# Blocks of four key tiles from the first head on, seven query products placed among the feed-forward groups, and the queries' scratch laid out by part

## The chip, the cores and the metric

The kernel runs on one core of a Trainium2 chip. The core has TensorE (PE, matmuls into PSUM), VectorE (DVE), ScalarE (ACT), GpSimd (POOL) and SyncE (SP), which here issues nearly all DMAs. Each engine runs its instructions in order and waits on semaphores for what others produce. The metric is the time of one execution on the device in microseconds (us), as a median over runs. The profile is of one further execution.

## The reference

The kernel computes a gated mix of an attention layer and a feed-forward layer over the same x (one batch, 2048 tokens, 512 features), all in float32:

```python
g = _sigmoid((x * gate_w).sum(-1, keepdims=True))
q = (x @ wq).reshape(B, S, 32, 16)      # 32 heads of 16
k = x @ wk;  v = x @ wv                 # one key and one value head, shared by all 32
p = softmax(einsum("bhqd,bkd->bhqk", q, k) * 16 ** -0.5)
a = einsum("bhqk,bkd->bhqd", p, v) -> (S, 512) @ wo
b = (silu(x @ w_gate) * (x @ w_up)) @ w_down      # hidden size 1792
out = g * a + (1 - g) * b
```

There is no mask. The output is 2048 x 512 in float32.

## The kernel before

**Precision.** Products in float32 are made of three matmuls: each operand is split into a high part of a shorter format and the rest (names ending in h and l), and hi x hi, hi x lo and lo x hi are summed in PSUM (`three`, L111). A weight tile arrives raw by DMA (`wraw`, two buffers), and POOL casts its high part (L107) and subtracts it (L108).

**Queries.** x is transposed into four chunks of 512 tokens (`XC[c]`, features on the partitions). A query product (m, c) multiplies columns 128 m to 128 m + 127 of wq, which are eight heads, with chunk c; there are 16. Of each result three parts are kept, the low part `ql`, the high part `qh` and a bound `qb` = kmax * |qh|, and written to a scratch in DRAM, `q_d` (L248). `load_head(h)` fetches one head's rows from there into `qs` (L665, L666): 128 partitions, that is twice four parts of 16 rows, for two halves of the query tokens, so that a score is one matmul per half with 64 rows (L680). For m = 0, ACT makes `qh` (L233) and `qb` (L234); for the others DVE makes all parts (L230 to L238). A reduction on DVE keeps each product's largest bound (L254).

**Three phases.** A setup transposes x, makes keys and values and the four query products of m = 0; head 0 gets its `qs` straight from them. `fill(GAP)` runs three more query products whole. The main phase follows, and then a tail with the feed-forward work that is left, the output projection with wo, and the sum.

**The main phase** is under a manual schedule: the order in which the code is written is the order on each engine. It goes through 512 units u, each one head and one of 16 key tiles. A unit has two scores S (each two matmuls into a PSUM tile `pss` of 128 x 1024, of which there are two buffers), the exponentials into `pt` (ACT, L688; of a score of kind "H", DVE copies one half out, L684, and ACT takes that half later), and a mix (L700: four matmuls, one per chunk of query tokens, that sum values and denominators in `po`; the profile records each as two). Between the scores stand steps F of other work, the jobs: a query product (12 steps), a gate or up product of one feed-forward tile and chunk (12), a down product of a group of tiles (15 or 12). A step is two matmuls with 64 rows each, the lower half of one job and the upper half of another (L192), which run side by side. `Halves` picks these jobs. What jobs leave to ACT and DVE stands in `ACTS` and `DEFER`, and `settle` or `block` runs it, `block` within a budget of DVE time.

**The order of units.** The first 32 units come in 16 blocks of two (four S, eight F, two units' mixes; `BEGIN`), since only three `pt` buffers fit beside the x chunks 2 and 3 and the weights of wq. When the last query product is done, these are given up (`open_acc`), and there are six buffers in two pools of three. One block of transition (`TURN`: ten scores, sixteen F) takes the order over to blocks of four units in the order of `STEPS`, with four units' mixes at the end of each.

**Jobs.** First the nine remaining query products, m by m; then for each chunk three groups of feed-forward tiles (5, 5 and 4), the gate and up products of a group interleaved with the down products of the group before. Gate and up weights are loaded for the next tile but one when a product ends. The first two of each, and the first group's down weights, are loaded ahead of the main phase (L785 to L790), on SP behind head 1's queries. Weights of the second chunk's pass are also stored split in `w_d` (L160) and read from there in later passes (L166).

Of the kernel before, what the change touches and what calls it, by code (L numbers as in the profile page):

```python
# [8 lines left out]
F32 = mybir.dt.float32  # L9
# [9 lines left out]
P = 128  # L19
# [27 lines left out]
PTB = 3  # L47
WRB = 2
BLOCK = 4
BEGIN = 16  # L50
STOP = 2
EARLY = 6
OUTS = (1, 2, 3, 0)
# [3 lines left out]
TURN = "SS" + "SFF" * 8  # L57
# [5 lines left out]
def tile_gated_mix(ctx, tc, x, wq, wk, wv, wo, w_gate, w_up, w_down, gate_w, out):  # L63
# [10 lines left out]
    q_d = dpool.tile([H, 3 * DH, S], F32, name="q_d")  # L74
# [19 lines left out]

    qpool = tc.alloc_tile_pool(name="qpool", bufs=1, side="right")
# [7 lines left out]
    ACC, PAIR = {}, []  # L103
# [19 lines left out]
    ACTS, DEFER, LOADS, HOLD, EVAC, FRESH = [], [], [], [], [], set()  # L123
# [87 lines left out]
    def load_wq(m):  # L211
        WQ[m] = load_split(wq_v[:, :, m * P:(m + 1) * P], f"wq{m}", 1, qpool)

    def query(m, c):
# [8 lines left out]

        def keep(ps):
            qh = wp.tile([P, CH], F32R, name="hh", bufs=7)
            ql = wp.tile([P, CH], F32R, name="hl", bufs=7)

            if m:
                qb = wp.tile([P, CH], F32, name="ht" if c % 2 else "hs", bufs=2)
                nc.vector.tensor_copy(qh, ps)  # L230
            else:
                qb = wp.tile([P, CH], F32R, name="hl" if c % 2 else "hh", bufs=7).bitcast(F32)
# [13 lines left out]
            def store():  # L246
                for j, part in enumerate(parts):
                    nc.sync.dma_start(q_d[m * HG:(m + 1) * HG, j * DH:(j + 1) * DH, cs], part.bitcast(F32))  # L248

            if m:  # L250
                store()
            else:
                STORES.append(store)
            nc.vector.tensor_reduce(top[:, t:t + 1], qb, axis=AX.X, op=ALU.max)  # L254

        return Job(3 * KD, lambda: m in WQ, terms, keep)

    def queries():
        jobs = [query(m, c) for m in range(1, KD) for c in range(NCH)]
        jobs[-1].after.append(open_acc)  # L260
        jobs[-1].after.append(lambda: nc.vector.tensor_reduce(top[:, KD * NCH:], top[:, :KD * NCH], axis=AX.X, op=ALU.max))
        return jobs

    def open_acc():
# [685 lines left out]
```

## Time and profile before

| | us |
| --- | --- |
| median of three runs (1341.17 to 1343.20) | 1342.19 |
| the profiled execution | 1340.92 |
| its span, first to last instruction | 1339.1 |
| TensorE busy in it | 1327.4 |
| ACT busy | 1069.0 |
| DVE busy | 710.3 |
| POOL busy | 220.3 |

A row of a timeline has start and duration in us, engine, line, operation, tiles (output, then inputs), partitions and shape, and in brackets how long the engine had been idle before and what released it. "x4" counts instructions that ran on without a gap. SPq is SP's queue: the duration there is that of the issue of a DMA, not of the transfer. The chain of waits is followed back from the last instruction; its rows are start, duration, and what ran. In a table by stretches a row has the stretch and its length, then busy time and instructions of PE, PE's weight loads, DVE, ACT and POOL, then the granted clock, the share of the 16 DMA engines in use, and GB/s.

### The profile page before, as it was taken

How to read it: one execution, taken by the hardware profiler on the slowest of the kernel's cores; microseconds unless marked ns; L12 is line 12 of the kernel's file. 1: busy time of each engine (PE TensorE's matmuls, PEld its weight loads, DVE VectorE, ACT ScalarE, POOL GpSimd, SP SyncE). 2: the span in 40 equal slices, each digit the busy share in tenths (PEclk: the TensorE clock that was granted, in tenths of full speed). 3: DMA queues.
4: the chain of work that ended last, by engine and by line, in shares of the span. 5: the costliest groups of instructions: out<-in, count | busy, mean ns of one | idle time of the engine just before them, and what ended most of it. 6: DMA issues, size and time to landing. Idle time of an engine off the chain costs nothing.

```text
span 1339.1 us, 26770 instructions
## 1 busy us (share of the span) xinstructions
PE 1327.4 (99%) x10743; PEld 769.7 (57%) x10743; DVE 710.3 (53%) x1221; ACT 1069.0 (80%) x1475; POOL 220.3 (16%) x228
## 2 busy tenths in 40 slices
PE   9999999999999999999999999999999999999998
PEld 7655555555555555555555555555555555555586
DVE  4555565465455555555555555455445565455442
ACT  4578888888888888888888888888888888888511
POOL 5141321152042141143020000000000000001223
PEclk9999999999999999999999999999999999999999
DMA  8455221131135372275162342243132342333154
GB/s 278 137 178 191 67 60 36 36 105 46 54 106 156 117 232 68 68 212 159 38 206 85 127 131 84 68 133 97 52 99 68 126 147 68 99 108 115 53 184 144
DMA packets 104178, 151.84 MB, mean 113 GB/s; under 512 B 12657, under 2 KB 43633, under 8 KB 102385
## 3 DMA queue, kind: packets, MB, share of 16 engines
q1 hardware_dynamic: 102320, 149.86, 36.4%
q8 instruction: 88, 1.44, 0.5%
q10 hardware_dynamic: 1728, 0.20, 0.1%
q14 instruction: 42, 0.34, 0.1%
HBM read 98.11 MB, written 51.38 MB: 112 GB/s over the span
## 4 chain that ended last, share of the span: by engine, by line
PE 98%; DVE 1%; ACT 1%; issue 0%; POOL 0%; DVEq 0%; ACTq 0%
PE pf L192 38%; PE po L700 34%; PE pss L680 21%; PE pf L117 4%; ACT pt L688 0%; PE pss L562 0%; PE po L549 0%; DVE xl L567 0%; PE pss L602 0%; DVE acc L345 0%; DVE hs L282 0%; POOL wul L108 0%; DVE wkv_l L108 0%; ACT xh L566 0%; DVE ot L464 0%
## 5 line engine op out<-in xcount | busy, mean ns | idle before, releaser
L688 ACT ACTIVATE pt<-pss 128x1024 f32<-128x1024 f32 (+1 forms) x1024 | 842.0, 876 | 177.7 <-PE pss L680 146.5
L684 DVE COPY pt<-pss 128x512 f32<-128x512 f32 x354 | 244.8, 691 | 421.4 <-PE pss L680 386.5
L700 PE MATMUL po<-pt,vaug 128*32 128x512 f32 x4096 | 467.6, 595 | 0.0
L680 PE MATMUL pss<-qs,ks 64*128 64x512 f32 x2048 | 402.4, 417 | 1.2 <-ACT pt L688 1.1
L680 PEld LDWEIGHTS pss<-qs,ks 64*128 64x128 f32 x2048 | 193.1, 184 | 218.7 <-ACT pt L688 183.5
L700 PEld LDWEIGHTS po<-pt,vaug 128*32 128x32 f32 x4096 | 119.2, 109 | 260.3 <-issue 255.2
L688 ACT ACTIVATE pt<-pt 128x512 f32<-128x512 f32 x354 | 195.7, 620 | 0.0
L192 PE MATMUL pf<-xh,wgl 64*128 64x512 f32 (+1 forms) x440 | 162.0, 391 | 0.0
L192 PE MATMUL pf<-xh,wgh 64*128 64x512 f32 (+1 forms) x440 | 160.8, 392 | 0.3
L192 PE MATMUL pf<-xl,wgh 64*128 64x512 f32 (+1 forms) x440 | 160.3, 390 | 0.0
L192 PE MATMUL pf<-xh,wuh 64*128 64x512 f32 (+1 forms) x440 | 158.3, 392 | 1.0 <-POOL wuh L107 0.5
L192 PE MATMUL pf<-xl,wuh 64*128 64x512 f32 (+1 forms) x440 | 158.1, 390 | 0.0
L192 PE MATMUL pf<-xh,wul 64*128 64x512 f32 (+1 forms) x440 | 157.1, 391 | 0.4 <-POOL wul L108 0.4
L192 PE MATMUL pf<-wdh,hl 64*128 64x512 f32 (+1 forms) x427 | 143.8, 390 | 0.0
L192 PE MATMUL pf<-wdh,hh 64*128 64x512 f32 (+1 forms) x427 | 143.3, 390 | 0.0
L192 PE MATMUL pf<-wdl,hh 64*128 64x512 f32 (+1 forms) x427 | 143.3, 390 | 0.0
L709 DVE RECIPROCAL rsb<-rsb 128x128 f32<-128x128 f32 x128 | 117.0, 935 | 10.1 <-issue 7.8
L447 POOL CAST xh<-wraw 128x512 fp32r<-128x512 f32 x4 | 2.9, 729 | 536.8 <-DMA wraw<-o_d 536.8
L192 PEld LDWEIGHTS pf<-xh,wgh 64*128 64x128 f32 (+1 forms) x440 | 78.5, 185 | 9.6 <-issue 1.3
L192 PEld LDWEIGHTS pf<-xh,wuh 64*128 64x128 f32 (+1 forms) x440 | 77.2, 185 | 9.7 <-issue 1.9
L192 PEld LDWEIGHTS pf<-xl,wgh 64*128 64x128 f32 (+1 forms) x440 | 78.5, 185 | 5.8
L192 PEld LDWEIGHTS pf<-xh,wgl 64*128 64x128 f32 (+1 forms) x440 | 78.5, 185 | 5.4
(158 smaller groups left out, 1361.5 us busy)
## 6 DMA issues: line engine op xcount, KB each, us to landing
qs<-q_d SPq DMA_DIRECT2D x62, 192.0 KB
wraw<-in_B_w_gate_dram SPq DMA_DIRECT2D x28, 256.0 KB
wraw<-in_B_w_up_dram SPq DMA_DIRECT2D x28, 256.0 KB
wraw<-in_B_w_down_dram SPq DMA_DIRECT2D x28, 256.0 KB
wgh<-w_d SPq DMA_DIRECT2D x28, 256.0 KB
wgl<-w_d SPq DMA_DIRECT2D x28, 256.0 KB
wuh<-w_d SPq DMA_DIRECT2D x28, 256.0 KB
wul<-w_d SPq DMA_DIRECT2D x28, 256.0 KB
```

Source lines behind the costliest of these rows:

```text
L117: nc.tensor.matmul(ps, a, b, start=(i == 0), stop=(i == n - 1))
L192: ins = nc.tensor.matmul(self.ps, a, b, start=(i == 0 and not half), stop=(last and half != 0))
L447: nc.gpsimd.tensor_copy(OT[c][0][:, k, :], raw)
L680: nc.tensor.matmul(ps[:, b * CH:(b + 1) * CH], ks[rows, kt * P:(kt + 1) * P], QS[h][rows, j, :], start=True, stop=True)
L684: other = nc.vector.tensor_copy(pt[:, CH:], ps[:, CH:]) if half else None
L688: ins = nc.scalar.activation(pt[:, w], ps[:, w], AF.Exp, scale=SCALE)
L700: nc.tensor.matmul(po[c * 2 * DH:(c + 1) * 2 * DH, :], vaug[:, kt, :], pt[:, c * CH:(c + 1) * CH], start=(kt == 0), stop=(kt == NT - 1))
L709: nc.vector.reciprocal(rsb[:, w], rsb[:, w])
```

## The change

- The main phase consists of blocks of four from the first unit on. An opening, `OPEN`, asks for the four scores of the first two units and eight F. The 16 blocks of two and the transition are gone. One pool of six `pt` buffers is there from the start.
- For that room, the chunks 2 and 3 of x and their pool are given up after `fill`, and the weights of wq lie in the three tiles that are later the feed-forward's accumulators (`HOME`; so at the start of the changed order `acc` stands for query weights).
- The query products come in another order. m = 0 is as before. `fill` runs the three of `EARLY_Q`, evacuated by ACT like m = 0. The two of `SECOND_Q` are the first jobs of the main phase, evacuated by DVE, their bound put off into `DEFER`. The seven of `LATE` stand behind the fifth job of seven feed-forward groups, in a pass that holds their chunk. Of a late product, `qh` has a buffer of its own, `ql` takes one of the two `osb` buffers that the heads' outputs use, and `qb` is computed in place over `qh` after that was stored, a block later (`SOON`).
- The scratch `q_d` is (3, 512, 2048), by part, instead of (32, 48, 2048), by head. A store writes 128 rows of 512; a head is fetched by eight DMAs of 16 x 2 x 512 instead of two of that size and two of 48 x 2 x 512.
- The load of wq's last part stands before the twelve stores of m = 0 instead of behind them; the reduction over the bounds' maxima stands in the tail.

```diff
-PTB = 3
+PTB = 6
-BEGIN = 16
+EARLY_Q = ((1, 2), (1, 3), (2, 3))
+SECOND_Q = ((1, 0), (1, 1))
+LATE = {(0, 0): (2, 0), (0, 1): (3, 0), (0, 2): (2, 1), (1, 0): (3, 1), (1, 1): (2, 2), (1, 2): (3, 2), (2, 0): (3, 3)}
-TURN = "SS" + "SFF" * 8
+OPEN = "SFSFFFSFFFSF"
...
-    q_d = dpool.tile([H, 3 * DH, S], F32, name="q_d")
+    q_d = dpool.tile([3, D, S], F32, name="q_d")
...
+    accp = tc.alloc_tile_pool(name="accp", bufs=3, side="right")
+    HOME = [accp.tile([P, TC, D], F32, name="acc") for _ in range(3)]
...
     def load_wq(m):
-        WQ[m] = load_split(wq_v[:, :, m * P:(m + 1) * P], f"wq{m}", 1, qpool)
+        home = HOME[2 if m > 1 else 1]
+        raw = wp.tile([P, KD, P], F32, name="wraw", bufs=WRB)
+        nc.sync.dma_start(raw, wq_v[:, :, m * P:(m + 1) * P])
+        WQ[m] = [home[:, m % 2 * 2 + j, :].rearrange("p (k n) -> p k n", k=KD).bitcast(F32R) for j in range(2)]
+        split(*WQ[m], raw, nc.gpsimd, nc.gpsimd)
...
+        late = (m, c) in LATE.values()
+        behind = late or (m, c) in SECOND_Q
         def keep(ps):
-            if m:
-                qb = wp.tile([P, CH], F32, name="ht" if c % 2 else "hs", bufs=2)
+            if late:
+                qh = hp.tile([P, CH], F32R, name="qh", bufs=1)
+                ql = hp.tile([P, CH], F32, name="osb").bitcast(F32R)
+                qb = qh.bitcast(F32)
...
+            if behind:
                 nc.vector.tensor_copy(qh, ps)
             else:
                 nc.scalar.activation(qh, ps, AF.Copy)
                 nc.scalar.activation(qb.bitcast(F32R), ps, AF.Abs, scale=kmax)
             nc.vector.tensor_tensor(ql, ps, qh.bitcast(F32), ALU.subtract)
-            if m:
-                nc.vector.tensor_scalar(qb, qh.bitcast(F32), kmax, None, op0=ALU.mult)
-                nc.vector.scalar_tensor_tensor(qb.bitcast(F32R), qb, -1.0, qb, op0=ALU.mult, op1=ALU.max)
...
-            def store():
-                for j, part in enumerate(parts):
-                    nc.sync.dma_start(q_d[m * HG:(m + 1) * HG, j * DH:(j + 1) * DH, cs], part.bitcast(F32))
+            def store(js=range(3)):
+                for j in js:
+                    nc.sync.dma_start(q_d[j, m * P:(m + 1) * P, cs], parts[j].bitcast(F32))
+            def scale():
+                nc.vector.tensor_scalar(qb, qh.bitcast(F32), kmax, None, op0=ALU.mult)
+            def bound():
+                nc.vector.scalar_tensor_tensor(qb.bitcast(F32R), qb, -1.0, qb, op0=ALU.mult, op1=ALU.max)
+                store([2])
+            def most():
+                nc.vector.tensor_reduce(top[:, t:t + 1], qb, axis=AX.X, op=ALU.max)
...
+            if behind:
+                store([0, 1])
+                (SOON if late else DEFER).extend([((m, c), 0.5, scale), ((m, c), 0.7, bound), ((m, c), 0.7, most)])
...
     def queries():
-        jobs = [query(m, c) for m in range(1, KD) for c in range(NCH)]
...
+        return [query(m, c) for m, c in EARLY_Q + SECOND_Q]
...
+                    if j == 4:
+                        if (m, GROUPS.index(fs)) in last:
+                            yield last[m, GROUPS.index(fs)]
...
+            load_wq(3)
             run(STORES, NCH)
-            load_wq(3)
             fill(GAP)
...
         def load_head(h):
-            qv = q_d[h].rearrange("r (j b s) -> b r j s", b=2, s=CH)
+            qv = q_d[:, h * DH:(h + 1) * DH, :].rearrange("i r (j b s) -> b i r j s", b=2, s=CH)
             for b in range(2):
-                nc.sync.dma_start(qs[b * RT:b * RT + DH], qv[b, DH:2 * DH])
-                nc.sync.dma_start(qs[b * RT + DH:(b + 1) * RT], qv[b])
+                for i, part in enumerate((1, 0, 1, 2)):
+                    row = b * RT + i * DH
+                    nc.sync.dma_start(qs[row:row + DH], qv[b, part])
...
             FRESH.clear()
+            DEFER.extend(SOON)
+            SOON.clear()
             for u in range(BLOCK * k, BLOCK * (k + 1)):
                 mix(u)
...
-            for n in range(BEGIN):
...
-            for k in range(2 * BEGIN // BLOCK, NB):
+            tiles = [(u, j) for u in range(2) for j in range(2)]
+            for what in OPEN:
+                if what == "S":
+                    exps(*score(*tiles.pop(0)))
+                else:
+                    feed(1)
+            for k in range(NB):
                 u = BLOCK * k
-                if k == 2 * BEGIN // BLOCK:
-                    n = u + 6 - (u + 1)
-                    block(k, u + 1, u + 6, TURN, "A" * 2 * n, [f"{i}d" for i in range(2 * n)])
```

Three places show instructions that moved. First SP, from the last but one store of a query product in `fill` on (`q_d<-`: stores of parts; `qs<-q_d`: the load of head 1; then the first gate and up weights). Before:

```order
L248 DMA q_d<-hl 8x16x512
L248 DMA q_d<-hh 8x16x512
L248 DMA q_d<-hs 8x16x512
L665 DMA qs<-q_d 16x2x512
L666 DMA qs<-q_d 48x2x512
L665 DMA qs<-q_d 16x2x512
L666 DMA qs<-q_d 48x2x512
L138 DMA wraw<-in_B_w_gate_dram 128x4x128
L138 DMA wraw<-in_B_w_up_dram 128x4x128
```

After:

```order
L264 DMA q_d<-hl 128x512
L264 DMA q_d<-hh 128x512
L264 DMA q_d<-ht 128x512
L698 DMA qs<-q_d 16x2x512 x8
L144 DMA wraw<-in_B_w_gate_dram 128x4x128
L144 DMA wraw<-in_B_w_up_dram 128x4x128
```

The number of stores ahead is the same in both, 21; their form is another, and the head's load is eight DMAs.

Second ACT, from the last evacuation of m = 0 on (`hh<-pf` is a copy, `<-pf,kmax` a bound, `pt<-pss` an exponential). Before:

```order
L233 ACTIVATE hh<-pf 128x512
L234 ACTIVATE hh<-pf,kmax 128x512
L233 ACTIVATE hh<-pf 128x512
L234 ACTIVATE hl<-pf,kmax 128x512
L688 ACTIVATE pt<-pss 128x1024 x66
```

After:

```order
L252 ACTIVATE hh<-pf 128x512
L253 ACTIVATE hl<-pf,kmax 128x512
L252 ACTIVATE hh<-pf 128x512
L253 ACTIVATE ht<-pf,kmax 128x512
L716 ACTIVATE pt<-pss 128x1024
L252 ACTIVATE hh<-pf 128x512
L253 ACTIVATE hs<-pf,kmax 128x512
L252 ACTIVATE hh<-pf 128x512
L253 ACTIVATE ht<-pf,kmax 128x512
L716 ACTIVATE pt<-pss 128x1024 x4
```

Two of the three early products are evacuated between the first exponential and the second.

Third TensorE, around the first product with gate weights (`wgh`, `wgl`), with what each instruction waits for. Before, where the lower half is gate work and the upper half the last query product:

```order
L192 MATMUL pf<-xh,wgh 128x512 [waits DVE_49,Pool_49]
L192 MATMUL pf<-xh_281,wq3l 128x512
L192 MATMUL pf<-xl,wgh 128x512
L192 MATMUL pf<-xh_281,wq3h 128x512
L680 MATMUL pss<-qs,ks 128x512 [waits Activation_49]
```

After, the first step of the second block of four:

```order
L728 MATMUL po<-pt,vaug 32x512 x2
L708 MATMUL pss<-qs,ks 128x512 [waits Activation_49]
L198 MATMUL pf<-xh,wgh 128x512 [waits Pool_49]
L198 MATMUL pf<-xl,acc 128x512
L198 MATMUL pf<-xl,wgh 128x512
L198 MATMUL pf<-xh,acc 128x512
L198 MATMUL pf<-xh,wgl 128x512 [waits Pool_49]
```

Before, 108 steps of query products come ahead of this one in the main phase; after, 24, and the upper half beside it (`acc`) is the second of the two remaining query products.

More of the change, by code (lines that the diff above doesn't have):

```diff
@@ L341, in add @@
             if c not in ACC:
-                ACC[c] = PAIR[0].tile([P, TC, D], F32, name="acc")
+                assert len(ACC) < 2 or not any(job in JOBS for job in last.values())
+                ACC[c] = accp.tile([P, TC, D], F32, name="acc")
             acc = ACC[c]
@@ L353, in store_acc @@
         nc.sync.dma_start(a_d[c], ACC[c])
+    last = {place: query(m, c) for place, (m, c) in LATE.items()}
     def jobs():
```

77 lines of the change are left out of this document (27 added, 50 removed).

## The prediction

> **What bounds the kernel now.** I read the page first, then TensorE's timeline at the start, then the chain of waits, and last the queue of SyncE (SP) and the copies of GpSimd (POOL) that feed the first feed-forward matmul.
>
> ```profile
> span 1339.1 us, 26770 instructions
> PE 1327.4 (99%) x10743; PEld 769.7 (57%) x10743; DVE 710.3 (53%) x1221; ACT 1069.0 (80%) x1475; POOL 220.3 (16%) x228
> PE 98%; DVE 1%; ACT 1%; issue 0%; POOL 0%; DVEq 0%; ACTq 0%
> ```
>
> TensorE is busy for 1327.4 of 1339.1 us and holds 98% of the chain that ended last. So only two things can move the end: TensorE's own work (the pattern in which it is laid out counts, since matmuls on the two row halves overlap), and the waits put in front of it. The change keeps the matmuls; what it alters is the pattern at the start and the waits. TensorE at the start, and its steady state in the chain of waits:
>
> ```profile
> 48.52 0.73 PE L680 MATMUL pss<-qs,ks 64*128 64x512 f32 x4
> 53.95 1.92 PE L700 MATMUL po<-pt,vaug 128*32 128x512 f32 x16
> 58.84 1.92 PE L700 MATMUL po<-pt,vaug 128*32 128x512 f32 x16
> ...
> 127.11 1.92 PE L700 MATMUL po<-pt,vaug 128*32 128x512 f32 x16
> 128.96 0.73 PE L680 MATMUL pss<-qs,ks 64*128 64x512 f32 x4
> 130.65 0.50 PE L680 MATMUL pss<-qs,ks 64*128 64x512 f32 x2 [0.95 <-ACT pt L688]
> 137.95 3.64 PE L700 MATMUL po<-pt,vaug 128*32 128x512 f32 x32
> ```
>
> ```profile
> 138.02 3.57 PE po L700 x32
> ...
> 345.92 3.57 PE po L700 x32
> ```
>
> The main phase begins with the score matmul at 48.52. Sixteen blocks of two key tiles follow, their mixes 4.88 us apart ((127.11 - 53.95) / 15), then the one block of transition, 10.84 us from mix to mix, 0.95 of it waiting for an exponential, then blocks of four. From 138.02 to 345.92 lie 22 of these: 9.45 us each.
>
> **The change, part by part: the start.** I compare up to the mix of the ninth block of four, which begins at 137.95 now. By then both orders have asked for the same 76 scores, 152 feed-forward steps and 32 mixed tiles, so a shift there is the shift of the end if the rest is left alone. Now two blocks of two take 2 x 4.88 = 9.76 where one of four takes 9.45: over 32 tiles (0.31 x 8) that is 2.5 us, and the transition costs 10.84 - 9.45 = 1.4. About 3.9 us are there to be won. Two things are put against it.
>
> **Exponentials behind evacuations.** ScalarE (ACT) now evacuates three more queries before the main phase, two of which stand between the first exponential and the second.
>
> ```profile
> 40.47 0.60 ACT L233 ACTIVATE hh<-pf 128x512 fp32r<-128x512 f32 x1 [1.54 <-PE pf L192]
> 40.97 0.68 ACT L234 ACTIVATE hl<-pf,kmax 128x512 fp32r<-128x512 f32 x1
> 49.22 3.77 ACT L688 ACTIVATE pt<-pss 128x1024 f32<-128x1024 f32 x4 [7.57 <-issue]
> ```
>
> A pair of evacuations takes 40.47 to 41.65, 1.18 us; an exponential 3.77 / 4 = 0.94. So the first exponential ends at 50.16, the two pairs at 52.52, the second to fourth at 53.46, 54.40 and 55.34. A score needs the buffer of the one two before it, so the second score of the first block of four waits until 55.34. What follows it is read from a normal block:
>
> ```profile
> 705.83 3.64 PE L700 MATMUL po<-pt,vaug 128*32 128x512 f32 x32
> 709.40 0.73 PE L680 MATMUL pss<-qs,ks 64*128 64x512 f32 x4
> 709.97 0.39 PE L192 MATMUL pf<-wdh,hh 64*128 64x512 f32 x1
> 715.19 3.64 PE L700 MATMUL po<-pt,vaug 128*32 128x512 f32 x32
> ```
>
> From the mix to the first step of the next block are 4.14 us, and from there to the next mix 9.45 - 4.14 = 5.31. The last two scores take 0.57, so one takes about 0.3: first step at 55.65, first mix at 60.9. Without the delay (2 x 1.18 = 2.36) it would be 58.6.
>
> **The first gate weights, a new wait.** The step that follows that mix, at 60.9 + 4.14 = 65.05, is the first product with `wgh`; now that product comes here, 46 us later:
>
> ```profile
> 110.97 0.39 PE L192 MATMUL pf<-xh,wgh 64*128 64x512 f32 x1
> ```
>
> Today nothing waits for these weights, because nine queries run first; the change leaves two, and the weights' load still stands behind 21 stores of queries and a head's load on SP. Its way today:
>
> ```profile
> 44.22 0.77 SPq L248 DMA_DIRECT2D q_d<-hl  x1
> 58.69 1.16 SPq L138 DMA_DIRECT2D wraw<-in_A_wq_dram  x1
> 69.96 1.13 SPq L248 DMA_DIRECT2D q_d<-hs  x1
> 71.13 1.22 SPq L665 DMA_DIRECT2D qs<-q_d  x1
> 74.29 1.26 SPq L666 DMA_DIRECT2D qs<-q_d  x1
> 75.66 0.53 SPq L138 DMA_DIRECT2D wraw<-in_B_w_gate_dram  x1
> 82.43 0.38 SPq L138 DMA_DIRECT2D wraw<-in_B_w_gate_dram  x1
> ```
>
> ```profile
> 80.41 0.61 POOL L107 CAST wgh<-wraw 128x512 fp32r<-128x512 f32 x1 [13.55 <-DMA wraw<-in_B_w_gate_dram]
> 81.10 1.30 POOL L108 TENSOR_TENSOR wgl<-wraw,wgh 128x512 fp32r<-128x512 f32 x1
> 86.01 0.61 POOL L107 CAST wgh<-wraw 128x512 fp32r<-128x512 f32 x1 [1.69 <-DMA wraw<-in_B_w_gate_dram]
> ```
>
> `wgh` is ready at 81.02: left so, TensorE would stand still for 16 us. But the stores get another layout. Their rate in the table by stretches (the last two columns are the DMA engines' share and GB/s), where the first row holds stores of 8x16x512 alone:
>
> ```profile
> 52.00:58.00 6.00, 6.00 (x47) 3.56 (x46) 4.32 (x8) 4.51 (x6) 0.00 (x0) 1.00 0.53 203
> 397.50:398.70 1.20, 1.20 (x14) 0.86 (x10) 1.18 (x2) 1.20 (x2) 0.24 (x1) 1.00 1.06 395
> 20.00:24.00 4.00, 4.00 (x27) 3.45 (x26) 2.53 (x3) 2.88 (x4) 3.29 (x5) 1.00 1.01 416
> 1269.00:1271.00 2.00, 2.00 (x10) 1.67 (x9) 1.97 (x4) 0.00 (x0) 1.17 (x1) 1.00 1.00 351
> ```
>
> ```profile
> 396.22 0.42 SPq L160 DMA_DIRECT2D w_d<-wgl  x1
> 50.03 0.69 DVE L230 CAST hh<-pf 128x512 fp32r<-128x512 f32 x1 [3.58 <-DMA q_d<-hh]
> ```
>
> The old stores fill half of the DMA engines: 262,144 bytes at 203 GB/s are 1.29 us. The second row holds two stores of the new form, 128x512 from 128 partitions (`w_d`): 395 GB/s, 0.66 us. The others are bounds: 416 GB/s (stores of x, 0.63) and 351 (loads of 128x512, 0.75). I take 0.68, near the row of the same form, with a little for a longer run of them.
>
> The Trainium skill, "DMA: Bandwidth & Descriptors", section "Why a DMA increments its semaphore by 16 and not by 1", has a rule for this: a transfer is spread over the largest number up to 16 that divides the slowest dimension of both patterns. That makes 8 engines for 8x16x512 and 16 for 128x512, and the traced 0.53 of the engines at 203 GB/s and 1.06 at 395 agree. By the rule alone, half of 1.29 would be 0.65, and the sum 0.6 us less than mine.
>
> The clock for the weights: the cast of `hh` that waited for the second store began at 50.03, so stores begin, completion included, from 50.03 - 2 x 1.29 = 47.45. The load of `wq3` goes ahead of them now: 0.75 by the row of loads, 48.2. Twenty-one stores at 0.68 end at 62.5. The last of eight head loads then has its semaphore free and is issued (0.6); from a gate load's issue to its cast are 3.6 us (82.43 to 86.01, short queue) or 4.75 (75.66 to 80.41, full queue). I take 4.0, since the up load comes right behind. With 0.61 for the cast: 62.5 + 0.6 + 4.0 + 0.61 = 67.7. TensorE waits 67.7 - 65.05 = 2.65 us. `wgl` is there 1.38 after `wgh` (81.02 to 82.40 today) and is asked for two steps, 0.46, later: 0.9 more. Bounds: 0.63 and 3.6 give 66.2; 0.75 and 4.75 give 69.9.
>
> **The sum.** Second mix at 67.7 + 0.9 + 5.31 = 73.9, seven blocks on (7 x 9.45 = 66.15) the ninth mix at 140.05, against 137.95: 2.1 us later. By the bounds: +0.6 to +4.3. Without the wait: 60.9 + 75.6 = 136.5, or 1.45 earlier; without the delayed exponentials either, 3.8 earlier.
>
> **What I cost at nothing.** Seven late queries: the same steps, in another place. VectorE (DVE) is busy 53%, and `scale`, which overwrites `qh`, comes one block (9.45 us) after the store was queued. Usually a store lands some 4 us after it is queued (3.6 from issue). If that cover is gone, DVE stands, behind it the copies of score tiles, and behind them TensorE; the price is under the rivals. A head's load becomes eight issues for four: 4 x 0.6 = 2.4 us more on SP per head, hidden since a head is loaded four blocks (37.8 us) ahead; what it moves is the weights behind it on SP. `wq3` is ready earlier. The reduction to the largest bound moves to the tail, on a DVE that has time. The second up and gate weights: 2 us behind the first on POOL, asked for 12 steps later. Six buffers from the start cost no instruction. For all of these together I allow 1.5 us to either side.
>
> So 1340.92 + 2.1 = 1343.0 for an execution like the one profiled (span 1339.1 and 1.8 around it). The median of the runs is 1342.19, 1.27 above it: 1344.3.
>
> **The rivals.** A measurement here can tell 0.2% (2.68 us) from no change.
>
> A, the forecast: +0.6 to +2.6, no change that can be told: 0.46.
>
> B, the weights come later than 68.3, and the same wait passes 2.68 us. For it: the spread of issue to cast (3.6 to 4.75), and 0.75 for a store. Against it: the row of the same form is at 0.66. +2.7 to +4.3, some 1345.7: 0.32, slower.
>
> C, the stores don't get faster: something other than their form holds them at 1.29. Then `wgh` stays at 81.0, the second mix comes at 87.2 and the ninth at 153.4: +15.4, 1357.6. For it: only two stores of the new form stand back to back in the trace. Against it: SP issued them 0.5 apart, so issuing isn't the limit. 0.05.
>
> D, SP's queue. Where it is full, a store is issued late:
>
> ```profile
> 467.92 1.18 DVE L712 TENSOR_TENSOR osb<-osb,rsb 128x512 f32<-128x512 f32 x1 [0.54 <-issue]
> ...
> 475.08 1.84 SPq L714 DMA_DIRECT2D o_d<-osb  x4
> ```
>
> The tile was done at 469.10 and its store issued 6.0 us later; with 3.6 to landing that is 9.6, beyond the block that covers `scale`. It decides from there on. Two of seven late queries with a stall of a whole landing, 3.6, give +7.2, or 1351.5 with the forecast's 2.1. The extra head issues (2.4 us) push the same way. 0.08, slower.
>
> E, a gain: the stores or the load are quicker, so that 65.05 is met, and waits further on ease, such as this one for POOL:
>
> ```profile
> 599.26 0.50 PE L192 MATMUL pf<-xh,wuh 64*128 64x512 f32 x1 [0.48 <-POOL wuh L107]
> ```
>
> Late queries put steps between groups, which gives weights time. 1.45, and about 1.4 from such waits, make -2.85: 1339.3. Against it: it needs stores of 0.55 us, 475 GB/s, above all rows. 0.09, faster.
>
> **How the numbers follow.** Likeliest is A, 1344.3, by itself 1342.8 to 1344.8. The range for 8 in 10 takes in E's 1339.3 on the one side and B and half of D on the other: 1339.3 to 1349.0; C and the worse of D lie outside. Faster 0.09 (E), same 0.46 (A), slower 0.45 (B, C, D).
>
> **What would show it.** In the new profile: stores of 128x512 issued 0.6 to 0.75 apart, the first gate load issued at 63 to 64; on ScalarE two pairs of evacuations between the first two exponentials; the first mix of 32 at 60.9; TensorE waiting for POOL's `wgh` and `wgl` near 65 to 69, 3.5 us in all; then mixes 9.45 apart, the ninth at 140. I am wrong if TensorE doesn't wait there, if the ninth mix is before 137 or after 143, or if blocks further on are longer than now, which would be D.

## The result and the profile after

The changed kernel takes 1365.42 us (median of five runs, 1362.48 to 1367.55), against 1342.48 for the kernel before. The recorded ratio over all runs is 1.0176, with a 95% interval of 1.0164 to 1.0188. The forecast was no change, 1344.3, with a range up to 1349.0; even the worst rival, 1357.6, lies below the result.

The page of the profiled execution. It took 1362.48 us, the shortest of the five, so some 3 us of the median's loss are in no trace:

```profile
span 1360.5 us, 27030 instructions
PE 1336.5 (98%) x10743; PEld 777.4 (57%) x10743; DVE 716.8 (53%) x1239; ACT 1076.2 (79%) x1508; POOL 218.9 (16%) x228
PEclk9899999999999999999999999999999999999999
PE 93%; DMA 2%; DVE 1%; ACT 1%; issue 1%; SPq 1%; POOL 1%; DVEq 0%; POOLq 0%
```

TensorE runs the same 10,743 matmuls, and is busy 9 us longer with them: the second of the 40 slices shows a granted clock below 0.9. TensorE's part of the chain fell from 98% to 93%, and DMAs, SP and POOL came into it. TensorE's timeline at the start, rows that answer to those shown of before:

```profile
52.69 0.80 PE L708 MATMUL pss<-qs,ks 64*128 64x512 f32 x2 [1.85 <-ACT pt L716]
63.78 3.64 PE L728 MATMUL po<-pt,vaug 128*32 128x512 f32 x32
72.88 0.79 PE L198 MATMUL pf<-xh,wgh 64*128 64x512 f32 x1 [4.80 <-POOL wgh L111]
80.22 3.64 PE L728 MATMUL po<-pt,vaug 128*32 128x512 f32 x32
...
146.82 3.64 PE L728 MATMUL po<-pt,vaug 128*32 128x512 f32 x32
```

The first mix is at 63.78 (forecast 60.9), the gate weights come at 72.88 (67.7), the second mix at 80.22 (73.9), the ninth at 146.82 (140.05; before 137.95). The table by stretches over the same time:

```profile
46.00:54.00 8.00, 6.12 (x27) 3.82 (x26) 2.47 (x4) 5.42 (x8) 1.89 (x2) 0.90 1.08 294
54.00:62.00 8.00, 7.80 (x29) 5.83 (x29) 2.13 (x4) 4.41 (x7) 0.00 (x0) 0.50 1.04 266
72.90:76.20 3.30, 3.17 (x14) 2.05 (x16) 0.00 (x0) 0.00 (x0) 3.10 (x3) 0.50 0.21 59
```

The granted clock was 0.50 from about 53 to 62 us and again from 72.9 to 76.2, after each of the two waits. The chain of waits tells why the weights came late:

```profile
56.76 8.20 DMA q_d<-hh
64.96 0.02 issue
64.98 1.30 SPq L698
...
68.23 0.59 SPq L698
...
68.93 3.24 DMA wraw<-in_B_w_gate_dram
...
72.22 0.62 POOL wgh L111
```

A store issued at 56.76 landed at 64.96, and only then could SP go on with the five of the head's loads that were left, most of them some 0.6 us each, up to the gate load at 68.93. How long the first and the last of the twenty-one stores took from issue to landing (last column; issued at 44.28 and 61.81):

```profile
q_d<-hl SPq DMA_DIRECT2D x1, 256.0 KB, 3.8
q_d<-ht SPq DMA_DIRECT2D x1, 256.0 KB, 6.0
```

So the first landed at 48.1 and the last at 67.8: 19.7 us for twenty more stores, 0.985 each.

**Where the rest is.** The ninth mix is 8.9 us later than before, the last one 20.8: from the ninth to the last are 1134.0 us now (146.82 to 1280.84) and were 1122.1 (137.95 to 1260.06). The 11.9 us are in three places. First, at every head:

```profile
734.54 3.64 PE L728 MATMUL po<-pt,vaug 128*32 128x512 f32 x32
743.89 3.64 PE L728 MATMUL po<-pt,vaug 128*32 128x512 f32 x32
753.45 3.64 PE L728 MATMUL po<-pt,vaug 128*32 128x512 f32 x32
762.87 3.64 PE L728 MATMUL po<-pt,vaug 128*32 128x512 f32 x32
```

The block in which a head's first score stands mostly takes 9.55 to 9.60 (here 743.89 to 753.45), the others 9.35 to 9.43. Before, it mostly took 9.44 to 9.47; TensorE's timeline of before:

```profile
762.15 3.64 PE L700 MATMUL po<-pt,vaug 128*32 128x512 f32 x32
771.62 3.64 PE L700 MATMUL po<-pt,vaug 128*32 128x512 f32 x32
```

With 30 heads that is 30 x 0.11 = 3.3 us. Second and third, single long blocks, whose waits TensorE's timeline names:

```profile
165.16 0.50 PE L198 MATMUL pf<-xh,wgh 64*128 64x512 f32 x2 [0.89 <-DVE ht L332]
...
281.23 0.46 PE L198 MATMUL pf<-xh,wgh 64*128 64x512 f32 x1 [1.57 <-DVE sign L447]
...
470.06 0.49 PE L198 MATMUL pf<-xh,wuh 64*128 64x512 f32 x1 [0.71 <-POOL wuh L111]
...
587.42 0.50 PE L198 MATMUL pf<-xh,wuh 64*128 64x512 f32 x1 [2.17 <-POOL wuh L111]
```

The blocks with waits for POOL's up weights take 11.00 and 13.85 us, so 1.55 and 4.4 over 9.45, of which the one at 599 us before (10.84, or 1.4 over) is to be taken off: 4.6. The blocks with waits for DVE, at 165 and 281 us, and one of 9.99 at 252 in which no wait is named, are 1.1, 1.8 and 0.5 over: 3.4. These make 3.3 + 4.6 + 3.4 = 11.3 of the 11.9. The tail is 0.6 us longer. SP's and POOL's timelines show what the up weights at 470 us were waiting for:

```profile
460.72 5.19 SPq L698 DMA_DIRECT2D qs<-q_d  x8
465.96 0.58 SPq L144 DMA_DIRECT2D wraw<-in_B_w_up_dram  x1
```

```profile
469.40 0.61 POOL L111 CAST wuh<-wraw 128x512 fp32r<-128x512 f32 x1 [7.18 <-PE pf L198]
```

Eight issues of a head's load keep SP for 5.19 us, and the up weights' load stands right behind them. POOL's row names TensorE for its idle time, but the load issued at 465.96 took 3.3 us and landed at 469.3, just ahead of the cast. At 587 us the up weights' load is the second weights' load behind eight such issues (575.37 to 581.12), issued at 582.74 and landed 3.9 later.

### The profile page after: what moved, and what is told of

Its sections match the earlier page's. It is cut to its first block, busy times and chain, and to the rows that moved or that the text cites. A ratio compares the mean times of both kernels' runs of the same rounds, so it can differ in the third digit from the quotient of the medians.

```text
span 1360.5 us, 27030 instructions
## 1 busy us (share of the span) xinstructions
PE 1336.5 (98%) x10743; PEld 777.4 (57%) x10743; DVE 716.8 (53%) x1239; ACT 1076.2 (79%) x1508; POOL 218.9 (16%) x228
## 4 chain that ended last, share of the span: by engine, by line
PE 93%; DMA 2%; DVE 1%; ACT 1%; issue 1%; SPq 1%; POOL 1%; DVEq 0%; POOLq 0%
PE pf L198 36%; PE po L728 33%; PE pss L708 20%; PE pf L121 3%; ACT pt L716 1%; SPq L698 1%; DMA q_d<-hh 1%; DMA wraw<-o_d 1%; PE pss L590 0%; DVE pt L712 0%; DMA wraw<-in_B_w_up_dram 0%; POOL xl L478 0%; PE po L577 0%; DMA wraw<-in_B_w_gate_dram 0%; DVE ht L322 0%
## 5 line engine op out<-in xcount | busy, mean ns | idle before, releaser
L716 ACT ACTIVATE pt<-pss 128x1024 f32<-128x1024 f32 (+1 forms) x1024 | 832.6, 864 | 190.3 <-PE pss L708 160.8
L712 DVE COPY pt<-pss 128x512 f32<-128x512 f32 x381 | 263.4, 691 | 472.2 <-PE pss L708 443.0
L708 PE MATMUL pss<-qs,ks 64*128 64x512 f32 x2048 | 411.7, 418 | 2.5 <-ACT pt L716 2.2
L708 PEld LDWEIGHTS pss<-qs,ks 64*128 64x128 f32 x2048 | 201.5, 185 | 213.5 <-ACT pt L716 170.5
L716 ACT ACTIVATE pt<-pt 128x512 f32<-128x512 f32 x381 | 210.7, 620 | 0.0
L198 PE MATMUL pf<-xh,wgh 64*128 64x512 f32 (+1 forms) x440 | 164.6, 394 | 7.9 <-POOL wgh L111 4.8
L198 PE MATMUL pf<-xh,wuh 64*128 64x512 f32 (+1 forms) x440 | 161.9, 393 | 3.1 <-POOL wuh L111 2.9
L198 PE MATMUL pf<-xh,wul 64*128 64x512 f32 (+1 forms) x440 | 162.4, 395 | 0.9 <-POOL wul L112 0.9
L198 PE MATMUL pf<-xl,wuh 64*128 64x512 f32 (+1 forms) x440 | 161.8, 393 | 0.0
L198 PEld LDWEIGHTS pf<-xh,wuh 64*128 64x128 f32 (+1 forms) x440 | 79.2, 185 | 12.2 <-POOL wuh L111 3.8
L198 PEld LDWEIGHTS pf<-xh,wul 64*128 64x128 f32 (+1 forms) x440 | 79.6, 186 | 7.6 <-POOL wul L112 1.7
```

The lines of the kernel that those rows point to most:

```text
L198: ins = nc.tensor.matmul(self.ps, a, b, start=(i == 0 and not half), stop=(last and half != 0))
L708: nc.tensor.matmul(ps[:, b * CH:(b + 1) * CH], ks[rows, kt * P:(kt + 1) * P], QS[h][rows, j, :], start=True, stop=True)
L712: other = nc.vector.tensor_copy(pt[:, CH:], ps[:, CH:]) if half else None
L716: ins = nc.scalar.activation(pt[:, w], ps[:, w], AF.Exp, scale=SCALE)
```

## The experiments

All times are medians, with the kernel before run on the same chip beside them (1340.3 to 1341.8).

**The scratch's layout alone.** The kernel before, with this and the stores and loads that belong to it:

```diff
-    q_d = dpool.tile([H, 3 * DH, S], F32, name="q_d")
+    q_d = dpool.tile([3, D, S], F32, name="q_d")
```

> The kernel before with nothing changed but the scratch of the queries (by part) and with it the form of its stores and the eight DMAs of a head's load. Theory of the head's load: eight issues keep SP busy for 5 to 6 us per head, weights queue up behind them, and TensorE waits for POOL in the second chunk's pass; four more semaphores to wait for delay the first score of every head by 0.11 us (30 x 0.11 = 3.3). Together +4 to +9 us, 1346.5 to 1351.5, every fourth block of four 0.1 longer than now. Rival, the late queries are what makes TensorE wait at 470 and 587 us: then the layout costs at most the 0.11 per head or nothing, 1342 to 1345.5.

Measured: 1346.06 against 1341.83, ratio 1.0033 (1.0017 to 1.0049), 4.2 us slower. Most blocks with a head's first score are 9.55 to 9.6. A new wait has come in the second chunk's pass, on TensorE and on SP:

```profile
494.16 0.50 PE L192 MATMUL pf<-xh,wuh 64*128 64x512 f32 x1 [1.74 <-POOL wuh L107]
```

```profile
485.02 5.01 SPq L666 DMA_DIRECT2D qs<-q_d  x8
490.07 0.59 SPq L138 DMA_DIRECT2D wraw<-in_B_w_up_dram  x1
```

So the new layout, with its eight issues, brings both costs even without late queries; where the issues meet a load of weights, TensorE waits.

**The first weights ahead of the stores.**

```diff
+            load_w("g", 0)
+            load_w("u", 0)
             load_wq(3)
             run(STORES, NCH)
```

> The changed kernel with the first gate and up weights' loads put ahead of the stores of the queries. Theory of the place in SP's queue: no wait for the gate weights any more, the second mix 9.45 us after the first, the ninth at 139.4 instead of 146.8; 7.4 us faster than the changed kernel, 1358.0. Rival, something else is nearly as late there (the second tile's weights, the evacuations): the wait moves, and less than 3 us are won, above 1362.

Measured: 1357.73, ratio 1.0127 (1.011 to 1.0144), 7.7 us less than the changed kernel. TensorE's timeline:

```profile
63.74 3.64 PE L730 MATMUL po<-pt,vaug 128*32 128x512 f32 x32
73.32 3.64 PE L730 MATMUL po<-pt,vaug 128*32 128x512 f32 x32
```

9.58 from first to second mix; the ninth is at 140.0. The place of these loads in SP's queue cost 7 us or so. The first mix is as late as ever, and the granted clock falls here too (0.50 from 53 us on), after pauses of only 0.17 and 0.42 us, in a stretch (51 to 53 us) in which TensorE was busy for 1.4 of 2 us. A wait of 1.62 us for DVE, at 56.27, comes after the clock has fallen.

**The old layout in the changed kernel.**

```diff
-    q_d = dpool.tile([3, D, S], F32, name="q_d")
+    q_d = dpool.tile([H, 3 * DH, S], F32, name="q_d")
```

> The changed kernel with the scratch by head again (stores of 8x16x512, a head's load of four DMAs). Theory: the gate weights come at about 81 and the ninth mix some 8 us later (155), but the head's boundary blocks are 0.1 shorter (-3.3) and the waits at 470 and 587 us shrink by some 4.5: 1365.6 in all, about the changed kernel's time. Rival, late queries cause those waits: they stay, 1370 to 1373.

Measured: 1371.39, ratio 1.023 (1.0213 to 1.0248). The rival's number was right. The profiled execution took 1366.08 us, so what follows leaves some 5 us of the median open. The gate weights come later still (TensorE waits 10.3 us for them, at 79.2), the blocks at heads are 9.46 again, but waits for up weights at 475, 593 and 710 us stay, of 1.0, 2.1 and 1.6 us. So four issues are also enough for a wait where the order of jobs brings them just ahead of weights. The changed order of jobs, which the late queries shift, takes part in that; the eight issues are not its only cause.

**Work in the gaps.** Matmuls that nobody reads, 8 in the first wait and 33 in the second:

```diff
+    def idle_work(ps, n):
+        for i in range(n):
+            nc.tensor.matmul(ps, ks[:, :P], QS[0][:, 0, :], start=(i == 0), stop=(i == n - 1))
...
+                    idle_work(ps_o.tile([P, CH], F32, name="po"), 8)
```

> The changed kernel with matmuls that nobody reads put into its first two waits of TensorE: 8 before the fourth score, 33 before the first product with gate weights. Theory, the granted clock falls because TensorE stands idle for about 1.9 us or more: the clock stays at 1.0 from 48 to 80 us, the first mix comes at 59 to 61 instead of 63.8, from the arrival of the gate weights to the second mix are 6.2 us instead of 7.3, and the ninth mix comes 1.1 us earlier; 1364.3. Rival, the clock falls for another reason (the load of those microseconds): it still falls to about 0.5 from 53 to 63 us and nothing is won.

Measured: 1364.68. The table by stretches and TensorE's timeline:

```profile
52.00:56.00 4.00, 3.54 (x18) 2.16 (x18) 1.86 (x4) 3.87 (x5) 0.00 (x0) 1.00 1.07 289
56.00:60.00 4.00, 4.00 (x30) 2.91 (x28) 1.50 (x4) 3.44 (x5) 0.00 (x0) 1.00 1.08 254
72.80:76.00 3.20, 1.75 (x12) 1.16 (x14) 0.00 (x0) 0.00 (x0) 2.87 (x4) 1.00 0.09 26
```

```profile
60.07 3.64 PE L736 MATMUL po<-pt,vaug 128*32 128x512 f32 x32
73.64 0.49 PE L206 MATMUL pf<-xh,wgh 64*128 64x512 f32 x1 [1.37 <-POOL wgh L111]
80.07 3.64 PE L736 MATMUL po<-pt,vaug 128*32 128x512 f32 x32
```

The clock stays at 1.0 and the first mix comes 3.7 us earlier, with the DMA engines as busy as in the changed kernel (1.07 and 1.08). The mean granted clock was 0.996 to 0.998 in all four executions, against 0.991 to 0.993 in the five of the changed kernel. So the missing work of TensorE had taken the clock. From the weights to the second mix are 6.4 us instead of 7.3. The weights came 0.8 later in this execution, and the end didn't move beyond what the runs scatter: behind late weights, an earlier first mix is worth nothing.

**Four variations on the early weights** (base 1357.73). First, a head fetched with four DMAs from the new layout:

```diff
-                for i, part in enumerate((1, 0, 1, 2)):
-                    row = b * RT + i * DH
-                    nc.sync.dma_start(qs[row:row + DH], qv[b, part])
+                nc.sync.dma_start(qs[b * RT:b * RT + DH], qv[b, 1])
+                nc.sync.dma_start(qs[b * RT + DH:(b + 1) * RT], qv[b])
```

> The changed kernel with the first weights' loads ahead of the stores (1357.7 us so far), and a head loaded by four DMAs out of the new scratch (16x2x512 and 48x2x512) instead of eight. Theory: the 0.11 us at each head's first score come from four more semaphores to wait for, so they go (30 x 0.11 = 3.3), and the shorter run of issues on SP eases the waits of TensorE for up weights at 464 and 583 us by half or so: 1351 to 1354.5, the block with a head's first score 9.46 instead of 9.57. Rival: those 0.11 us come from the data's way or the burst has nothing to do with the waits: 1357 or so, blocks of 9.57 stay.

Measured: 1371.37, ratio 1.023 (1.0213 to 1.0247), far slower. The blocks at heads are 9.46 to 9.48, as the theory wanted, but SP's queue is worse off:

```profile
460.15 0.77 SPq L699 DMA_DIRECT2D qs<-q_d  x1
460.96 0.46 SPq L144 DMA_DIRECT2D wraw<-in_B_w_up_dram  x1
```

```profile
470.08 0.79 PE L198 MATMUL pf<-xh,wuh 64*128 64x512 f32 x1 [3.62 <-POOL wuh L111]
```

Up weights issued at 460.96 were of use 9.1 us later. Two 48x2x512 loads, whose source's slowest dimension is now 3, go before them. The first, issued at 458.65, landed only at 465.16; the up weights landed at 469.30, 8.3 us after their issue, against 3.3 in the changed kernel. By the rule that the prediction cited (the Trainium skill, "DMA: Bandwidth & Descriptors", section "Why a DMA increments its semaphore by 16 and not by 1") such a load would be on 3 engines. The trace agrees: the semaphore events of the first are one jump at 459.86 and then three landings, at 464.67, 464.81 and 465.16; those of a 16x2x512 load or a 128x512 store are sixteen.

Second, the eight DMAs spread over three blocks:

```diff
-                if k % (NT // BLOCK) == 0 and 0 < h < H - 1:
-                    load_head(h + 1)
+                if k % (NT // BLOCK) < 3 and 0 < h < H - 1:
+                    load_head(h + 1, range(8)[k % (NT // BLOCK) * 3:][:3])
```

> The same base (1357.7), with a head's eight DMAs spread over three blocks, 3, 3 and 2, instead of issued in one run. Theory of the burst: weights queue behind 5 to 6 us of issues on SP, so now the waits for up weights at 464 and 583 us (blocks of 12.88 and 12.90) are gone, 6 to 7 us less: 1351; the blocks with a head's first score stay at 9.57. Rival: the waits come from the late queries' stores or from the stores of split weights in that pass: they stay, 1357.

Measured: 1361.85, ratio 1.0155 (1.0139 to 1.0172), 4 us slower than the base. The waits for up weights at 464 and 583 us are gone, which is the theory of the burst. But some heads' first scores now wait for the third part of their queries, at six places, such as this:

```profile
476.61 0.58 PE L711 MATMUL pss<-qs,ks 64*128 64x512 f32 x1 [2.36 <-DMA qs<-q_d]
```

Third, two early queries on DVE (`behind` for them too):

```diff
-        behind = late or (m, c) in SECOND_Q
+        behind = late or (m, c) in SECOND_Q + EARLY_Q[1:]
```

> The same base (1357.7), with the second and third early query evacuated by DVE instead of ACT (DVE makes the parts as for the other queries). Theory: exponentials no longer stand behind evacuations, TensorE has no long wait before its first mix, the granted clock stays at 1.0 there, the first mix comes at 59 instead of 63.74 and everything behind it 4.5 us earlier: 1353. Rival: DVE is late instead (its copies of score tiles behind 6 us of evacuations, which wait for stores), the first mix comes at 61 to 63 and 1 to 3 us are won: 1355 to 1357.

Measured: 1357.52, no change; the first mix at 63.43. The wait was for the stores of m = 0, whose buffers the early queries take over, and these stood behind the weights: moving the weights ahead had made them late, on either engine (the first is issued at 49.02 us here and at 44.28 in the changed kernel).

Fourth, `BUDGET = 5.0` for 3.8:

> The same base (1357.7), with the DVE budget of a block raised from 3.8 to 5.0. Theory: the blocks of 10.58 at 160, of 11.24 at 275 and of 9.98 at 245 us are long because the product of tanh and gate was pushed out of its block by the heads' reciprocals and stands ahead of an up product's evacuation, for whose PSUM buffer TensorE waits; with the larger budget it runs in its block, and these are 9.4 to 9.5: some 3 us less, 1354.8. Rival: longer DVE work at the ends of blocks delays the copies of score tiles; other blocks get longer, and nothing is won.

Measured: 1357.47, no change by the median. But in the profiles the stretch from the ninth mix to the last takes 1131.4 us (141.66 to 1273.04) against 1134.9 (140.01 to 1274.92), 3.5 less, and the waits for DVE at 158 and 274 us are gone. In that execution the start was 1.6 later. The two blocks and the one behind the first take 29.0 instead of 31.4; the block of 9.98 at 245 us stays, and the waits for up weights moved too. So the theory holds for two of its three blocks, with some 2.4 us, and the gain is not shown in the time.

**All repairs together.** The budget, DVE for the two early queries, heads in two runs of four, and the weights behind the six stores whose buffers are needed first:

```diff
+            run(STORES, 2)
+            load_w("g", 0)
+            load_w("u", 0)
             load_wq(3)
             run(STORES, NCH)
```

> The changed kernel with four repairs: the first gate and up loads after the first six stores instead of behind all (the early queries' buffers wait for those six), second and third early query evacuated by DVE, a head's eight DMAs in two runs of four a block apart, and a DVE budget of 5.0. If the causes found so far are all: first mix at 59 to 60, ninth at 136, no wait for up weights in the second chunk's pass, none at 160 and 275 us; 1365.4 - 7.7 (weights) - 3.9 (first mix) - 6.5 (burst) - 3.5 (budget) = 1343.8, and what is left above the kernel before are the 3.3 us of the heads' first scores. Rival, the repairs collide or the late queries have a cost of their own: over 1350.

Measured: 1350.09, ratio 1.0076 (1.0051 to 1.0101). The first mix is at 58.08 and the late waits are gone, but the second tile's gate weights now come late, 6.3 us at 80.7.

> The same with the early queries evacuated by ACT, as in the changed kernel. Theory of the exponentials behind evacuations: the first mix 2 to 3.5 us later than with DVE, at 62 to 63, and 2 to 4 us slower than that kernel. Rival, only the stores that the evacuations wait for matter and not the engine: the same within 1 us.

Measured: 1352.0, by the medians 1.9 slower than with DVE; the intervals of the two (1.0066 to 1.0109 and 1.0051 to 1.0101) overlap. The first mix is at 64.39, behind a wait of 1.85 for an exponential at 54. Evacuations between the exponentials cost the first mix 6.3 us, and nearly all of that is swallowed by the second tile's weights: the ninth mix is at 143.66, with DVE at 143.40.

> The four repairs with DVE, with the scratch by head again (four DMAs per head, stores of 8x16x512) and the second tile's first loads also ahead of the early queries' stores. Theory: the heads' first scores are not delayed (-3.3), stores are slow but nothing waits for them: some 1340, level with or just below the kernel before. Rival: early queries wait for the slow stores of m = 0 (1.29 each), TensorE stands still and its clock falls: 1346 to 1350.

Measured: 1359.85, ratio 1.0147 (1.012 to 1.0175); waits of 5.4 us for DVE at 80.6 and 4.1 for gate weights at 105. DVE, in turn, had waited for a store to free its buffer:

```profile
77.94 0.49 DVE L267 TENSOR_SCALAR ht<-hh,kmax 128x512 f32<-128x512 f32 x1 [9.84 <-DMA q_d<-ht]
```

In this order the slow stores aren't hidden.

The second tile's loads also ahead of the early queries' stores:

```diff
             run(STORES, NCH)
+            load_w("g", 1)
+            load_w("u", 1)
             fill(GAP)
```

> The four repairs with DVE, and the second tile's first gate and up loads also ahead of the early queries' stores. Theory: the wait of 6.3 us at 80.7 and the slow clock behind it are gone, the ninth mix comes at 135 to 136 instead of 143.4, the rest stays: 1341.5 to 1343 against 1350.1; what is left against the kernel before are about 3 us won at the start and 3.3 lost at the heads' first scores. Rival, another late load takes its place (down weights, early queries' stores): 1346 or more.

Measured: 1347.68, ratio 1.005 (1.0032 to 1.0068); the lowest median of all variants of the change, still slower than the kernel before, and 5 us more than expected. TensorE's timeline:

```profile
58.46 3.64 PE L733 MATMUL po<-pt,vaug 128*32 128x512 f32 x32
68.10 3.64 PE L733 MATMUL po<-pt,vaug 128*32 128x512 f32 x32
75.10 0.50 PE L713 MATMUL pss<-qs,ks 64*128 64x512 f32 x2 [1.07 <-DVE pt L717]
...
94.94 0.50 PE L198 MATMUL pf<-xh,wgh 64*128 64x512 f32 x2 [1.38 <-POOL wgh L111]
96.30 0.50 PE L198 MATMUL pf<-xh,wgl 64*128 64x512 f32 x2 [0.62 <-POOL wgl L112]
```

Blocks of 11.67 and 11.94 us remain here. Against the kernel before, its span is 6.6 us longer: 1.0 at the ninth mix (138.92), 4.6 from there to the last mix, 3.3 of them the heads' first scores, and 1.0 in the tail.

**Half of the semaphores elsewhere.** One short matmul at a job's start reads the next head's queries first:

```diff
+                while TOUCH:
+                    nc.tensor.matmul(self.ps[:, :64], ks[:RT, :P], QS[TOUCH.pop()][:RT, 0, :64], start=True, stop=True)
```

> The same, and at the first job that begins two blocks ahead or more, one short matmul of 64 columns reads the lower half of the next head's queries into a PSUM tile that is then overwritten, so that four of the eight semaphores are waited for there and not at the head's first score. Theory of the semaphores: the blocks with a head's first score are 9.46 or shorter instead of 9.57, 2 to 3 us less than without: 1339 to 1341. Rival, the delay comes from the data's way or moves to the new matmul: the same within 1 us.

Measured: 1349.83, by the medians 2.1 slower, with intervals that overlap (1.0049 to 1.0084). The blocks at heads stay at 9.54 to 9.64, and the blocks ahead of them, mostly 9.35 to 9.43 without it, are mostly 9.44 to 9.53. The rival: nothing is saved. That eight DMAs per head go with 9.57 and four with 9.46 is the same in all kernels here; that it is the number of semaphores is not.

**The kernel before, a head's loads in two runs of two.**

> The kernel before, with each head's four DMAs in two runs of two, a block apart. Theory of the burst: TensorE's waits of 0.48 and 0.41 for up weights at 599 us are gone, 1.4 us less (the block there is 10.84 instead of 9.45): about 1340. Rival: nothing changes, or the first scores of heads now wait: 1341.5 or more.

Measured: 1341.32 against 1340.34, ratio 1.0004 (0.9995 to 1.0014), no change. The block at 600 us is 9.92 instead of 10.84; a microsecond is below what the runs can tell.

**What a stall costs.** The kernel before, with six waits made by a reduction whose result is not used:

```diff
+            if k in SITES:
+                red = nc.vector.tensor_reduce(junk, XC[3][0].rearrange("p k c -> p (k c)").bitcast(F32)[:, :SITES[k]], axis=AX.X, op=ALU.max)
+                follow(red, LASTS[0])
+                HELD.append(red)
```

> The kernel before with six made stalls, one in every fourth block from the 75th to the 95th: the block's first mix waits for a reduction on DVE over 500, 900, 1200, 1450, 1700 and 2000 elements that begins when the block's last score ends (its result goes unused). TensorE should stand idle some 0.6, 1.0, 1.3, 1.6, 1.8 and 2.1 us. Theory, the clock follows the length of one idle gap, with a limit between 1.57 and 1.85: the first four cost what they last (10.0, 10.4, 10.7, 11.0 us per block), the last two 1.5 to 3 us more, with a granted clock of 0.5 for 3 us or more behind the gap. Rival, what counts is the work in a stretch before (the kernel's start has half of the array idle): none of the six makes the clock fall, and each costs its length.

It took 1363.25 us in one execution. The gaps came out longer than meant: 1.88, 1.65, 2.11, 3.06, 3.85 and 2.90 us. TensorE's timeline and the table by stretches behind three of them:

```profile
885.34 3.64 PE L704 MATMUL po<-pt,vaug 128*32 128x512 f32 x32 [3.06 <-DVE junk L789]
...
927.55 5.34 PE L704 MATMUL po<-pt,vaug 128*32 128x512 f32 x32 [3.85 <-DVE junk L789]
...
969.78 4.96 PE L704 MATMUL po<-pt,vaug 128*32 128x512 f32 x32 [2.90 <-DVE junk L789]
```

```profile
885.30:888.00 2.70, 2.66 (x28) 0.86 (x32) 0.00 (x0) 0.00 (x0) 0.00 (x0) 1.00 0.92 343
...
927.50:930.00 2.50, 2.45 (x16) 0.71 (x20) 0.00 (x0) 0.00 (x0) 0.00 (x0) 0.62 0.00 0
...
969.70:972.00 2.30, 2.22 (x12) 0.59 (x16) 0.02 (x1) 0.02 (x1) 0.00 (x0) 0.50 0.08 21
```

Gaps of 1.65, 1.88, 2.11 and 3.06 us cost what they last (to within 0.4 us, by the blocks' lengths), and the clock stays. Those of 2.90 and 3.85 bring it to 0.5 for some 2.5 to 4 us, and with the block behind them they cost 1.8 and 2.0 us more than they last. A limit on the length of one gap, which I had between 1.57 and 1.85, does not exist. At the changed kernel's start the clock fell after a gap of 1.85, in a stretch where most steps use half of the array's rows and the array has pauses anyhow; no run shows which of the two counts. Nor do pauses and busy time alone decide: the two of 0.17 and 0.42 us, with TensorE busy for 1.4 us of 51 to 53, stood before a fall with the early weights alone, and with all repairs and the second tile's loads the same pauses and the same 1.4 us left the clock at 1.00.

## Why the prediction was wrong

**What bounds the kernel, and where the new wait would be**, were right: TensorE did wait for `wgh` in the second block, the early evacuations did delay the second exponential, and the order held. The size was wrong, and two parts that I costed at nothing were not nothing. The ninth mix came 6.8 us later than forecast: 5.1 of these are the gate weights, 1.1 the slow clock behind them, and 0.5 the seven blocks that follow. Behind it, and in the tail, are 12.5 us for which I had nothing, with 1.5 allowed to either side.

**The gate weights (67.7, measured 72.83).** The step that failed is the term "twenty-one stores at 0.68", which ends at 62.5. That rate was read from two stores of `w_d`; the twenty-one landed 0.985 us apart, and the last one at 67.8, 5.3 us after the forecast, though the first landed 0.8 earlier than I had it. The head's issues took another 0.5 beyond the one that I counted: the gate load went out at 68.93 instead of 63.1. From there to the end of the cast it took 3.9 instead of 4.6, which gave 0.7 back. Why the rate fell is open: the run is longer, and the rows also go elsewhere, since `w_d`'s 128 rows of 2 KB lie one behind the other and `q_d`'s lie 8 KB apart; no run separates the two. The form of the stores did make them faster (10.3 us of wait with the old one against 4.8), so rival C was rightly small.

**The clock, for which the sum had no term.** I priced a wait of TensorE at its length. The wait of 1.85 us for the second exponential was in the sum, and the score behind the fourth exponential even came earlier than forecast, at 54.60 instead of 55.34. But some 10 us at half clock followed: that is how the first mix came at 63.78, not 60.9. Work put into the gap removes it (60.07). That loss is hidden behind the later weights. The same after 72.88: 7.34 to the second mix, not 6.2, and this one counts.

**What I costed at nothing.** "Hidden since a head is loaded four blocks ahead" looked at the head's queries and not at what stands behind them on SP, though I named it. With the burst of eight issues came the waits at 470 and 587 us (gone when it was split, though four issues and the changed order make some too), and every head's first score came some 0.11 us later. Rival D had the queue and the sign right, but as the cost of late queries' stores, with a chance of 0.08; none of the waits seen is for `scale`.

**DVE's budget, not thought of.** With jobs at another place in the blocks, the product of tanh and gate fell out of the budget in two blocks, and TensorE waited: 2.9 us, of which a larger budget won back 2.4 in the one trace of it. The third long block, 0.5 us over, is not explained.

**The gain** is shown in no run. With the weights in place and the evacuations off ACT, the first mix does come at 58.1 to 58.5 (I had 58.6 without the delay), but the best variant's ninth mix is at 138.92, still 1.0 later than before. Its two long blocks, 11.67 and 11.94, are 4.7 over 9.45; without them the ninth mix would be 3.7 earlier than before, close to the 3.8 that I had. That is a sum and not a measurement.

Still open: what the seven late queries cost by themselves, beyond shifting the jobs; and why eight DMAs delay a head's first score more than four.

## What to carry to other kernels

A gain in the pattern of the bound engine is worth what the queues behind it allow: before moving a consumer ahead, walk its whole supply with a rate read from a run as long as the real one and into the same kind of rows, and with every issue that stands ahead on the queue. Price a stall of TensorE as its length and, if it is about 2 us or longer, possibly some 2 us more for a slow clock behind it, as here; more where its work comes thinly. Splitting one transfer into two is free only if nothing urgent stands behind it on its queue.

## What the hardware showed that was not expected

The granted clock fell after idle gaps of 1.85, 2.17, 2.90, 3.85 and 4.80 us, and did not after 1.57, 1.65, 1.88, 2.11 and 3.06. So a gap's length alone doesn't decide. The Trainium skill, "TensorE: Matmul & The Clock Gate", section "What's actually happening", has a free-running activity window of about 3.4 us behind this, so that it matters where in the window a gap lies; 3.06 without a fall beside 2.90 with one agrees with that, while falls after 1.85 and 2.17, and one after pauses of only 0.17 and 0.42, show that a window need not be wholly idle.

Stores of 128x512 with 2 KB rows ran at 395 GB/s when two came alone, into rows that lie one behind the other, and at 266 to 294 in a row of twenty-one into rows 8 KB apart, with the DMA engines' share at 1.04 to 1.08 in each: the engines as busy, but for longer per byte.
